# One weight row taken past the second expert product: precomputed token factors in a fused linear attention and soft mixture of experts kernel

## The chip, the cores and the metric

The kernel runs on one core of a Trainium2 chip. The metric is the device time of one execution in microseconds (us); the median of several executions counts. The profile is one execution recorded by the hardware profiler; its span (119.8 us before the change) runs from the first to the last instruction and is a little shorter than the device time of the same execution (121.55 us).

## The reference

Two layers run one after the other. The first is a linear attention with a decaying state for 4 batches, 8 heads, 768 tokens and head size 48. Its output, seen as `x` of 3072 tokens by 384 features, feeds a soft mixture of 8 experts with 4 slots each:

```python
logits = x @ phi                              # 3072 x 32
d = exp(logits - max over tokens); d /= d.sum(0)
slot_input = (d.T @ x).reshape(8, 4, 384)
for e in range(8):
    h = np.maximum(slot_input[e] @ w1[e], 0.0)   # 4 x 1024
    slot_out[e] = h @ w2[e]                      # 4 x 384
c = exp(logits - max over slots); c /= c.sum(1)
out = c @ slot_out.reshape(32, 384)           # 3072 x 384
```

The last line is linear in `slot_out`, and `slot_out` of one expert is a sum over the 1024 rows of its `w2`. So the contribution of some rows of `w2` can be added either to `slot_out` or, after a product with the token weights, straight to `out`. That is what the change uses.

## The kernel before

Everything is one straight program; the helper `O` keeps every engine's instructions in the order in which they are written. The attention and the dispatch part of the mixture fill the span up to about 90 us and are not touched. The change concerns what follows.

**Weights.** All expert weights are loaded by GpSimd-issued transfers that convert float32 to bfloat16 on the way: eight pieces `w1_all[:, e]`, then `w2` of experts 0 to 6 whole, and `w2` of expert 7 in three pieces (L576, L577). The 1024 rows of one `w2` lie as 128 partitions by 8 "rows" `y`, so piece `(y0, y1)` carries rows `y0` to `y1 - 1` of every partition. `w2` of all experts lands in the tiles `raw`.

**First expert product** (L619 to L631). The hidden values of 4 experts at a time (group `g`, 32 partitions per expert) go into two banks of PSUM per group, named by `hb`; ScalarE or VectorE applies the maximum with zero and writes `h_sb`. TensorE transposes `h_sb` (L648) into `hT`.

**Second expert product** (`second`, L656). It adds, for each row `y`, each half `x` of the 384 columns and each expert `j`, one product of 32 stationary columns by 192 columns into the banks `SO[0]` (tile `Xb`) and `SO[1]` (tile `Yb`). The order is: group 0, experts 4 and 5, one filler product `busy(1)` (L144), expert 6, expert 7. Expert 7 comes last because its weights land last.

**Slot outputs.** After it come four small products that sum token weights (`row_sums(8, 12)`, L637), then `so` (L671 on VectorE, L672 on ScalarE), which scales the two banks by `csr`, the reciprocal of the column sums of `d`, and writes bfloat16.

**Output** (`emit`, L682). There are 24 output tiles; tile `i` holds tokens `i, i + 24, ...` in 128 partitions by 384 columns. One TensorE product of the transposed token weights `LexpT[:, i:Nn:nN]` (128 by 128) with `so` fills one of six PSUM banks, and VectorE (even tiles, L686) or ScalarE (odd tiles, L688) scales it by the reciprocal row sum `rsr` into SBUF. The first two tiles are cut into two halves so that both engines work on them. After tile 5 and after tile 11 stand six more `row_sums` products with their reciprocal (L641).

Finished tiles leave in groups of 1, 1, 2, 2, 2, 4, 4, 4 and 4 tiles, one transfer each (L704). Groups 1, 2, 3, 5, 7 and 9 are issued by SyncE, groups 4, 6 and 8 by GpSimd:

```python
sizes = [1, 1, 2, 2, 2, 4, 4, 4, 4]
...
O((sp, pool)[gi % 2 if gi > 1 else 0].dma_start(out=out_v[:, i0:i, :], in_=o_s))
```

Of the kernel before, what the change touches and what calls it, by code (L numbers as in the profile page):

```python
# [9 lines left out]
def kernel(  # L10
# [14 lines left out]
    C = 128  # L25
    nC = S // C
    Nn, Dm = out.shape
    ES = moe_phi.shape[1]
    E = moe_w1.shape[0]
# [3 lines left out]
    nF = F // C  # L33
# [5 lines left out]
    nN = Nn // C  # L39
# [6 lines left out]
    f32 = mybir.dt.float32  # L46
    bf = mybir.dt.bfloat16
    i32 = mybir.dt.int32
    AF = mybir.ActivationFunctionType
    ALU = mybir.AluOpType  # L50

    def O(ins):
        return tc.keep_in_program_order(ins)

    pe, dve, act, pool, sp = nc.tensor, nc.vector, nc.scalar, nc.gpsimd, nc.sync

    big = ctx.enter_context(tc.tile_pool(name="big", bufs=1))
    cst = ctx.enter_context(tc.tile_pool(name="cst", bufs=1))
# [6 lines left out]
    EG = E // 2  # L65
    raw = [big.tile([128, 3 * RW], f32, name=f"raw{j}") for j in range(NR)]
    eW2 = nF * Dm
    w1_all = big.tile([128, E, nM, F], bf, name="w1_all")

    def w2_of(e):  # L70
        g, j = divmod(e, EG)
        return raw[1 + g][:].bitcast(bf)[:, j * eW2:(j + 1) * eW2].rearrange("p (y d) -> p y d", y=nF)
# [4 lines left out]
    T0 = psb.tile([128, 1024], bf, name="T0")  # L77
    T1 = psb.tile([128, 1024], bf, name="T1")
    Ab = psb.tile([128, 2, 512], f32, name="Ab")
# [3 lines left out]
    Vb = psb.tile([128, 512], f32, name="Vb")  # L83
# [9 lines left out]
    LexpT = cst.tile([128, Nn], bf, name="LexpT")  # L93
# [39 lines left out]
    def load_w(n, y0=0, y1=nF):  # L133
        if n < E:
            O(pool.dma_start(out=w1_all[:, n, :, :],
                             in_=moe_w1[n].rearrange("(p mo) f -> p mo f", p=128)))
        else:
            O(pool.dma_start(out=w2_of(n - E)[:, y0:y1, :],  # L138
                             in_=moe_w2[n - E].rearrange("(p y) d -> p y d", p=128)[:, y0:y1, :]))

    def keep_warm(n, bank=Yb, data=None):
        data = warm if data is None else data
        for _ in range(n):
            O(pe.matmul(bank[:, 0:512], data[:, 0:128], data[:, 0:512], start=True, stop=True))  # L144
# [349 lines left out]
    for i in range(-5, nH):  # L494
# [50 lines left out]
        if i in Z_AT:  # L545
            q = Z_AT[i]
# [12 lines left out]
        if i == 6:  # L559
            for mi in range(nM):  # L560
                for j in range(nM):
# [4 lines left out]
                                start=(j == 0), stop=(j == nM - 1)))  # L566
# [6 lines left out]
            load_w(nw)  # L573
            nw += 1
    assert nw == 2 * E - 1
    for y0, y1 in ((0, 4), (4, 7), (7, 8)):  # L576
        load_w(nw, y0, y1)  # L577


# [2 lines left out]
    Ab0 = Ab[:, 0, :]  # L582

    def busy(n):
        keep_warm(n, Ab[:, 1, :], w1_all[:, 0, 0, :])
# [23 lines left out]
    csr = cst.tile([128, 1], f32, name="csr")  # L609
# [4 lines left out]
    hb = [[Ab0, Vb[:]], [Yb[:], Ab[:, 1, :]]]  # L614
    FH = F // 2
    PH = C // 2
    h_sb = [Wf[0].bitcast(bf)[:, g * F:(g + 1) * F].rearrange("p (y c) -> p y c", c=C) for g in range(2)]
    hT = [Wf[1].bitcast(bf)[:, g * F:(g + 1) * F].rearrange("p (y c) -> p y c", c=C) for g in range(2)]
    for g in range(2):  # L619
        for a in range(2):  # L620
            for mi in range(nM):
                for j in range(EG):
                    O(pe.matmul(hb[g][a][32 * j:32 * j + 32, 0:FH], uns[:, mi, g, j, :],
                                w1_all[:, g * EG + j, mi, a * FH:(a + 1) * FH],
                                start=(mi == 0), stop=(mi == nM - 1), skip_group_check=True))
            src = hb[g][a][:, 0:FH].rearrange("p (q y) -> p y q", y=nF)
            dst = h_sb[g][:, :, a * PH:(a + 1) * PH]
            if a == 0:
                O(act.activation(out=dst, in_=src, func=AF.Relu))
            else:  # L630
                O(dve.tensor_scalar(out=dst, in0=src, scalar1=0.0, scalar2=None, op0=ALU.max))  # L631

    rsr = cst.tile([128, nN], f32, name="rsr")

    def row_sums(a, z):
        for i in range(a, z):
            O(pe.matmul(Mb[:, i:i + 1], LexpT[:, i:Nn:nN], ones[:, 0:1],  # L637
                        start=(i == a), stop=(i == z - 1), skip_group_check=True))

    def row_recip(a, z):  # L640
        O(dve.reciprocal(rsr[:, a:z], Mb[:, a:z]))  # L641

    HD = Dm // 2
    NY = nF // 2
    tb = [[T0[:], T1[:]], [Ab0.bitcast(bf), Vb[:].bitcast(bf)]]
    for g in range(2):
        for y in range(nF):
            O(pe.transpose(tb[g][y // NY][:, (y % NY) * C:(y % NY + 1) * C], h_sb[g][:, y, :], ident[:]))  # L648
        O(act.copy(hT[g][:, 0:NY, :].rearrange("p y c -> p (y c)"), tb[g][0][:, 0:NY * C]))
        O(dve.tensor_copy(hT[g][:, NY:nF, :].rearrange("p y c -> p (y c)"), tb[g][1][:, 0:NY * C]))  # L650
        if g == 0:
            row_sums(0, 8)
    row_recip(0, 8)
    SO = [Xb[:, 0:HD], Yb[:, 0:HD]]

    def second(g, experts):  # L656
        for y in range(nF):
            for x in range(2):
                for j in experts:
                    O(pe.matmul(SO[x][32 * j:32 * j + 32, :], hT[g][:, y, 32 * j:32 * j + 32],  # L660
                                w2_of(g * EG + j)[:, y, x * HD:(x + 1) * HD],
                                start=(g == 0 and y == 0), stop=(g == 1 and y == nF - 1), skip_group_check=True))

    second(0, range(EG))
    second(1, range(EG - 2))
    busy(1)
    second(1, (EG - 2,))
    second(1, (EG - 1,))
    row_sums(8, 12)
    so = Wf[1].bitcast(bf)[:, 2 * F + nM * ES * 8:2 * F + nM * ES * 8 + Dm]  # L670
    O(dve.tensor_scalar_mul(so[:, 0:HD], SO[0], csr[:, 0:1]))  # L671
# [7 lines left out]
             Wf[0][:, 2 * Dm:4 * Dm]]  # L679
            + [raw[0][:, x * 4 * Dm:(x + 1) * 4 * Dm] for x in range(4)])  # L680

    def emit(i, bank, dst, x0, x1, eng):  # L682
        op = ob[bank % 6][:, 0:x1 - x0]
        O(pe.matmul(op, LexpT[:, i:Nn:nN], so[:, x0:x1], start=True, stop=True))
        if eng is dve:
            O(dve.tensor_scalar_mul(dst[:, x0:x1], op, rsr[:, i:i + 1]))  # L686
        else:
            O(act.activation(out=dst[:, x0:x1], in_=op, func=AF.Copy, scale=rsr[:, i:i + 1]))  # L688

    i = 0  # L690
    for gi, sz in enumerate(sizes):
        o_s = obuf[gi][:, 0:sz * Dm].rearrange("p (n m) -> p n m", m=Dm)
        i0 = i
        for j in range(sz):
            if i < 2:
                emit(i, 2 * i, o_s[:, j, :], 0, HD, dve)
                emit(i, 2 * i + 1, o_s[:, j, :], HD, Dm, act)
            else:
                emit(i, i + 2, o_s[:, j, :], 0, Dm, (dve, act)[i % 2])
            i += 1  # L700
            if i in (6, 12):
                row_sums(i + 6, i + 12)
                row_recip(i + 6, i + 12)
        O((sp, pool)[gi % 2 if gi > 1 else 0].dma_start(out=out_v[:, i0:i, :], in_=o_s))  # L704
# [30 lines left out]
```

The softmax here doesn't subtract the row's maximum and nothing guards it: scores larger than these inputs give would overflow.

## Time and profile before

| | before |
|---|---|
| device time, median of 3 (range) | 121.68 us (121.32 to 121.8) |
| span of the profiled execution | 119.8 us |
| busy share of the span: TensorE / VectorE / ScalarE / GpSimd | 85% / 81% / 70% / 49% |
| granted TensorE clock, mean | 0.959 of full |
| bytes moved by transfers | 31.79 MB, mean 265 GB/s |
| share of the last chain that is the wait for `w2` | 34% |

The busy shares are means over stages with quite different limits. Read the end of the span by time instead: the last weights land a little after 102 us, the slot outputs are made around 103.5 us, TensorE and the two scaling engines produce output tiles from 104 to 111 us, and the output transfers go on until 117.5 us. The last 2.3 us up to 119.8 us hold no transfer and no compute.

### The profile page before, as it was taken

How to read it: one execution, taken by the hardware profiler on the slowest of the kernel's cores; microseconds unless marked ns; L12 is line 12 of the kernel's file. 1: busy time of each engine (PE TensorE's matmuls, PEld its weight loads, DVE VectorE, ACT ScalarE, POOL GpSimd, SP SyncE). 2: the span in 40 equal slices, each digit the busy share in tenths (PEclk: the TensorE clock that was granted, in tenths of full speed). 3: DMA queues.
4: the chain of work that ended last, by engine and by line, in shares of the span. 5: the costliest groups of instructions: out<-in, count | busy, mean ns of one | idle time of the engine just before them, and what ended most of it. 6: DMA issues, size and time to landing. Idle time of an engine off the chain costs nothing.

```text
span 119.8 us, 4336 instructions
## 1 busy us (share of the span) xinstructions
PE 102.0 (85%) x1797; PEld 82.0 (68%) x1797; DVE 96.4 (81%) x187; ACT 83.9 (70%) x183; POOL 59.2 (49%) x70
## 2 busy tenths in 40 slices
PE   5994977799999999999999999999998998896000
PEld 1453866687888888889878798888785696683000
DVE  6899999999999999899999899999954420399000
ACT  4459769797988898988988997998882520398000
POOL 7328634599999999788677595011000000013000
PEclk9998699999999999999999999999999999999955
DMA  2999999999999999999999999999999998179992
GB/s 83 255 370 374 373 367 369 363 391 367 339 381 385 348 229 215 213 213 217 213 217 213 217 218 215 212 217 212 217 215 217 211 209 161 23 274 383 410 410 99
DMA packets 20925, 31.79 MB, mean 265 GB/s; under 512 B 1129, under 2 KB 17898, under 8 KB 20906
## 3 DMA queue, kind: packets, MB, share of 16 engines
q0 software_dynamic: 2960, 14.55, 55.5%
q1 hardware_dynamic: 17920, 16.96, 41.8%
q8 instruction: 14, 0.23, 0.7%
q14 instruction: 5, 0.04, 0.1%
q10 hardware_dynamic: 26, 0.00, 0.0%
HBM read 39.38 MB, written 4.72 MB: 368 GB/s over the span
## 4 chain that ended last, share of the span: by engine, by line
DMA 34%; PE 28%; DVE 17%; issue 6%; ACT 3%; POOL 3%; POOLq 0%; DVEq 0%; ACTq 0%
DMA raw<-in_moe_w_dram 34%; PE Vb L284 4%; PE T L235 3%; DVE W L188 3%; DVE prod L257 3%; PE Ab L299 3%; PE Yb L352 2%; POOL kr L228 2%; DVE AT L304 2%; PE T L247 2%; PE Mb L325 2%; DVE kn L252 2%; DVE Z L341 2%; PE Yb L144 2%; PE Yb L365 1%
## 5 line engine op out<-in xcount | busy, mean ns | idle before, releaser
L228 POOL TENSOR_TENSOR kr<-raw,W 128x576 bf16<-128x576 f32 x30 | 42.2, 1428 | 13.8 <-ACT W L192 6.2
L304 DVE TENSOR_TENSOR AT<-Ab,mask_ut 128x768 bf16<-128x768 f32 x32 | 30.3, 946 | 0.8 <-PE Ab L299 0.6
L235 PE MATMUL T<-ident,kr 128*128 128x128 bf16 x192 | 16.8, 227 | 1.8 <-POOL kr L228 1.7
L284 PE MATMUL Vb<-v_bf,Q 128*128 128x96 bf16 x288 | 17.8, 208 | 0.0
L284 PEld LDWEIGHTS <-Q 128*128 128x128 bf16 x288 | 15.9, 99 | 1.5 <-issue 0.2
L241 ACT COPY kT<-T 128x768 bf16<-128x768 bf16 x16 | 12.8, 800 | 4.6 <-PE T L235 3.3
L241 ACT COPY rT<-T 128x768 bf16<-128x768 bf16 x16 | 12.8, 801 | 4.2 <-PE T L235 3.6
L257 DVE TENSOR_TENSOR prod<-T,kT 128x768 bf16<-128x768 bf16 x16 | 15.2, 948 | 0.0
L235 PEld LDWEIGHTS <-kr 128*128 128x128 bf16 x192 | 12.5, 101 | 2.6 <-POOL kr L228 1.9
L342 DVE TENSOR_TENSOR dv<-vn,Mb 128x288 bf16<-128x288 bf16 x32 | 14.1, 440 | 0.0
L290 ACT CAST vn<-Vb 128x288 bf16<-128x288 f32 x32 | 13.4, 419 | 0.1
L341 DVE TENSOR_TENSOR Z<-Mb,zt 128x288 bf16<-128x288 f32 (+1 forms) x32 | 12.7, 397 | 0.6
L372 ACT CAST x<-Yb 128x288 bf16<-128x288 f32 x32 | 13.1, 409 | 0.1
L299 PE MATMUL Ab<-rT,kT 64*128 64x128 bf16 x192 | 11.1, 222 | 2.1 <-DVE AT L304 2.0
L704 POOL DMA_DIRECT2D out_dram<-W x1 | 0.6, 552 | 24.2 <-DVE W L686 24.2
L325 PE MATMUL Mb<-vn,kn 128*128 128x96 bf16 (+2 forms) x80 | 11.5, 242 | 0.0
L352 PE MATMUL Yb<-vn,AT 128*128 128x48 bf16 x192 | 10.3, 185 | 0.1
L270 ACT CAST v_bf<-raw 128x576 bf16<-128x576 f32 x15 | 10.2, 678 | 0.0
L299 PEld LDWEIGHTS <-kT 64*128 64x128 bf16 x192 | 5.6, 95 | 5.6 <-DVE AT L304 2.0
L352 PEld LDWEIGHTS <-AT 128*128 128x128 bf16 x192 | 7.1, 96 | 3.3
L138 POOL DMA_DIRECT2D raw<-in_moe_w_dram x10 | 5.5, 558 | 7.8 <-DMA raw<-in_moe_w_dram 7.7
L365 PE MATMUL Yb<-dv,ident 128*128 128x288 bf16 x32 | 9.1, 284 | 0.2
(143 smaller groups left out, 221.3 us busy)
## 6 DMA issues: line engine op xcount, KB each, us to landing
w_all<-in_moe_w_dram POOLq DMA_DIRECT2D x8, 768.0 KB, 12.9
raw<-in_moe_w_dram POOLq DMA_DIRECT2D x7, 768.0 KB, 18.2
raw<-in_v_dram SPq DMA_DIRECT2D x12, 288.0 KB, 6.6
raw<-in_k_dram SPq DMA_DIRECT2D x8, 288.0 KB, 6.0
raw<-in_r_dram SPq DMA_DIRECT2D x8, 288.0 KB, 6.2
raw<-in_k_dram SPq DMA_DIRECT2D x2, 1152.0 KB, 12.3
raw<-in_r_dram SPq DMA_DIRECT2D x2, 1152.0 KB
out_dram<-raw POOLq DMA_DIRECT2D x2, 768.0 KB, 6.9
```

The source lines that it names most:

```text
L228: O(eng.tensor_mul(kr[:, j].rearrange("p j (h s) -> p j h s", s=64)[:, :, :, 0:D], src, W[j][:, q].rearrange("p j (h d) -> p j h d", h=2)))
L235: O(pe.transpose(bank[:, x * C:(x + 1) * C], kr[:, j, x, :], ident[:]))
L241: O(act.copy(t[:].rearrange("p (s j) -> p s j", j=J), bank[:, 0:S].rearrange("p (j s) -> p s j", j=J)))
L257: O(dve.tensor_mul(pr[:].rearrange("p (s j) -> p s j", j=J), T1[:, 0:S].rearrange("p (j s) -> p s j", j=J), st["kT", m][:].rearrange("p (s ...
L284: O(pe.matmul(Vb[:, c * P2:(c + 1) * P2], Q3[:, o:o + C], vb[:, :, g, j, :], start=(j == 0), stop=(j == JV - 1)))
L290: O(act.copy(vn[:].rearrange("p c e d -> p (c e d)"), Vb[:, 0:L * P2]))
L299: O(pe.matmul(Ab[:, e, c * C:(c + 1) * C], kT[s, t], rT[s, t]))
L304: O(dve.tensor_mul(AT[:], Ab[:, :, 0:T].rearrange("p e (c t) -> p e c t", c=L), mask_ut[:, None, None, :].to_broadcast([128, 2, L, C])))
L325: O(pe.matmul(o, kn[:, g * L + c, :], vc, start=first, stop=True, skip_group_check=True))
L341: O(dve.tensor_mul(Z[:], Mb[:, 0:x * P2].rearrange("p (c e) -> p c e", c=x), zt[:, q, 0:x, :]))
L342: O(dve.tensor_mul(dv[:], st["v", i][:].rearrange("p c e d -> p (c e) d"), Mb[:, 288:288 + 2 * L, None].to_broadcast([128, L * 2, D])))
L352: O(pe.matmul(Yb[:, o:o + D], AT[:, e, c, :], vn[:, c, e, :], start=first, stop=False, skip_group_check=True))
```

## The change

The last row (`y = 7`) of expert 7's `w2` no longer passes through the second expert product. Instead:

- `hs` holds the hidden values that multiply this row (those of the last 32 partitions, scaled by `csr`), made by two small ScalarE instructions (`hs_half`) from the same PSUM banks as before.
- `g_last(q)` multiplies `hs` with the token weights in token order, 512 tokens at a time; the six results, 128 partitions by 3072 tokens, go as bfloat16 into `gl`, which takes the place of expert 7's `w1`. ScalarE copies three of them out of PSUM and VectorE three. The first takes the place of `busy(1)`, the other five stand between experts 6 and 7.
- `second` for expert 7 runs over rows 0 to 6 only.
- Every output tile becomes the sum of two products in one PSUM bank: first `gl` of its tokens with row 7 of `w2`, then, as before, the token weights with `so`. For the first two tiles the four half-tile products of the first kind are issued ahead of all products of the second kind; from tile 2 on the two stand together.
- The three pieces of the last expert's `w2` become 5, 2 and 1 rows in place of 4, 3 and 1.

The purpose is that the piece of weights that lands last need not go through the second product and the scaling into `so` before output can start.

```diff
-    for y0, y1 in ((0, 4), (4, 7), (7, 8)):
+    for y0, y1 in ((0, 5), (5, 7), (7, 8)):
         load_w(nw, y0, y1)
...
+    last = slice(32 * (EG - 1), 32 * EG)
+    hs = cst.tile([128, C], bf, name="hs")
+
+    def hs_half(a):
+        O(act.activation(out=hs[last, a * PH:(a + 1) * PH], in_=hb[1][a][last, nF - 1:FH:nF], func=AF.Relu,
+                         scale=csr[last, 0:1]))
+
+    hs_half(0)
+    gl = w1_all[:, E - 1, :, :].rearrange("p m f -> p (m f)")
+    GW = 512
+    gbank = [Ab[:, 1, :], T0[:].bitcast(f32), T1[:].bitcast(f32), Ab0, Vb[:], Ab[:, 1, :]]
+
+    def g_last(q):
+        O(pe.matmul(gbank[q], hs[last, :], LexpT[last, q * GW:(q + 1) * GW], start=True, stop=True))
+        dst = gl[:, q * GW:(q + 1) * GW]
+        if q % 2:
+            O(dve.tensor_copy(dst, gbank[q]))
+        else:
+            O(act.copy(dst, gbank[q]))
...
+    hs_half(1)
     row_recip(0, 8)
...
-                                start=(g == 0 and y == 0), stop=(g == 1 and y == nF - 1), skip_group_check=True))
+                                start=(g == 0 and y == 0),
+                                stop=(g == 1 and y == nF - 1 - (j == EG - 1)), skip_group_check=True))
 
     second(0, range(EG))
     second(1, range(EG - 2))
-    busy(1)
+    g_last(0)
     second(1, (EG - 2,))
-    second(1, (EG - 1,))
+    for q in range(1, 6):
+        g_last(q)
+    second(1, (EG - 1,), range(nF - 1))
     row_sums(8, 12)
...
-    def emit(i, bank, dst, x0, x1, eng):
+    def emit(i, bank, dst, x0, x1, eng, first=True, then=True):
         op = ob[bank % 6][:, 0:x1 - x0]
-        O(pe.matmul(op, LexpT[:, i:Nn:nN], so[:, x0:x1], start=True, stop=True))
+        if first:
+            O(pe.matmul(op, gl[:, i:Nn:nN], w2_of(E - 1)[:, nF - 1, x0:x1], start=True, stop=False))
+        if not then:
+            return
+        O(pe.matmul(op, LexpT[:, i:Nn:nN], so[:, x0:x1], start=False, stop=True))
...
+    for i in range(2):
+        for x in range(2):
+            emit(i, 2 * i + x, None, x * HD, (x + 1) * HD, None, then=False)
...
-                emit(i, 2 * i, o_s[:, j, :], 0, HD, dve)
-                emit(i, 2 * i + 1, o_s[:, j, :], HD, Dm, act)
+                emit(i, 2 * i, o_s[:, j, :], 0, HD, dve, first=False)
+                emit(i, 2 * i + 1, o_s[:, j, :], HD, Dm, act, first=False)
```

More of the change, by code (lines that the diff above doesn't have):

```diff
@@ L652, with second @@
             row_sums(0, 8)
+    hs_half(1)
     row_recip(0, 8)
     SO = [Xb[:, 0:HD], Yb[:, 0:HD]]
-    def second(g, experts):
-        for y in range(nF):
+    def second(g, experts, ys=range(nF)):
+        for y in ys:
             for x in range(2):
```

## The prediction

> **What bounds the kernel now.** I read the chain that ended last first, in order of time, because the change concerns only the end of the span. Columns are start, length and what was running.
>
> ```profile
> 77.84 24.80 DMA raw<-in_moe_w_dram
> 102.64 0.04 issue
> 102.68 0.24 PE Xb L660
> ...
> 103.33 0.10 PE Xb L660
> 103.43 0.02 issue
> 103.46 0.43 DVE W L671
> 103.89 0.04 issue
> 103.93 0.33 PE T L684 x2
> ```
>
> The middle piece of the last `w2` (rows 4 to 6) lands at 102.64 us and releases TensorE; eight products follow at about 0.082 us each (102.68 to 103.25), so row 7 must have landed by 103.17 without being waited for. VectorE makes half of `so` in 0.43 us, and the first output product starts at 103.93 us.
>
> Second, the transfers from 105 to 113 us, in slices of 0.2 us:
>
> ```profile
> DMA  0009999999999999999599919989899989899979
> GB/s 0 0 8 338 353 323 353 361 415 415 384 369 461 354 323 415 384 384 569 215 461 492 430 62 461 399 338 430 369 461 461 399 338 430 338 492 461 369 307 399
> ```
>
> From 105.6 us on, the output transfers keep all transfer engines busy, except for one hole, at 109.6 us (62 GB/s). Windows cut at that hole (from and to, length, busy time of TensorE, its weight loads, VectorE, ScalarE and GpSimd, granted clock, transfer share, GB/s):
>
> ```profile
> 105.40:107.40 2.00, 2.00 (x18) 1.85 (x18) 2.00 (x6) 2.00 (x6) 0.55 (x1) 1.00 0.90 332
> 107.40:109.60 2.20, 1.97 (x10) 1.13 (x8) 2.20 (x6) 2.20 (x6) 0.53 (x1) 1.00 1.05 408
> 109.60:109.80 0.20, 0.20 (x2) 0.00 (x0) 0.20 (x2) 0.20 (x1) 0.00 (x0) 1.00 0.19 62
> 109.80:113.80 4.00, 0.03 (x1) 0.00 (x0) 1.07 (x3) 0.65 (x2) 0.53 (x1) 0.94 1.01 406
> 113.80:117.40 3.60, 0.00 (x0) 0.00 (x0) 0.00 (x0) 0.00 (x0) 0.00 (x0) 0.50 1.02 418
> ```
>
> Groups 1 to 5 are 8 tiles of 196,608 bytes. Groups 6 to 9 are the other 16, 3.15 MB, and start at 109.8 us; at about 410 GB/s they take 7.7 us, which gives the 117.5 us where transfers stop. So the end is set by when group 6 (tiles 8 to 11) can start. Third, the timeline around it:
>
> ```profile
> 105.75 0.33 PE L684 MATMUL Xb<-W,LexpT 128*128 128x384 bf16 x1
> 105.91 0.33 PE L684 MATMUL Yb<-W,LexpT 128*128 128x384 bf16 x1
> ...
> 106.89 0.58 ACT L688 ACTIVATE raw<-T,rsr 128x384 f32<-128x384 f32 x1
> ...
> 107.04 0.61 DVE L686 TENSOR_SCALAR raw<-T,rsr 128x384 f32<-128x384 f32 x1
> ...
> 108.22 0.53 POOL L704 DMA_DIRECT2D out_dram<-raw x1 [1.06 <-ACT raw L688]
> ```
>
> TensorE gives a tile every 0.16 us; VectorE needs about 0.525 us per even tile (107.04 to 107.65 is tile 10), ScalarE about 0.47 per odd one (106.89 to 107.47 is tile 11). Tile 10 closes group 6 at 107.65 us, GpSimd's record starts at 108.22, and its bytes flow from 109.8, 1.6 us later. Group 4's record starts at 106.60; a window from 104.7 to 108.5 us lists SyncE's queue alone, and one from 108.5 to 109.7 lists 0.39 MB, just group 4, on GpSimd's: 2.0 us. So group 6 came at the short end of what this path takes, without visible slack: a delay of tiles 8 to 11 moves the end one for one.
>
> **What the Trainium skill says.** "TensorE: Matmul & The Clock Gate", Back-to-back issue gap, gives N / 2.4 + 2.5 ns for a warm product of N columns: 162 ns at 384, and the trace has 0.16 us. "VectorE: DVE Perf Modes", Why PSUM operands drop a tier, says a float32 operand in PSUM gets no fast mode; the trace agrees: 192 columns take 0.42 us and 384 take 0.61, about 1 ns per column. "DMA: Bandwidth & Descriptors", Issuing engines are not separate DMA queues, says that all issuers share 16 transfer engines: spreading over SyncE and GpSimd adds no bandwidth, as the steady 406 to 418 GB/s shows. Its section Latency and other measured facts has about 1 us to the first byte for GpSimd's path; the trace's 1.6 and 2.0 us are longer and are used.
>
> **The change part by part.**
>
> *Pieces of 5, 2, 1.* Same bytes. From 101.35 us (rows 0 to 3 landed, by the wait of TensorE before 101.39) to 102.64 three rows came, 0.43 us each. So rows 0 to 4 land at about 101.8, rows 5 and 6 still at 102.64, row 7 at about 103.1 (102.64 + 0.43). After 102.64 only four products of the second kind remain in place of eight: 4 x 0.082 = 0.33 us less, if TensorE is free then.
>
> *Making `hs` and `gl`.* `hs_half(0)` falls on ScalarE at 94.9, where it idles 0.36 us; about 0.25 us for 64 columns (0.42 less 128 x 1 ns, bounded by 0.42) hides there. `hs_half(1)` comes at 96.9 and ScalarE is idle until 103.5. `g_last(0)` replaces `busy(1)` one for one. Five `g_last` follow expert 6, whose last product starts at 100.73: 5 x 0.21 = 1.07 us (512 columns at the rate of the 384), plus about 0.1 us for each switch between product shapes (the 99.16 filler and the step from 103.25 to 103.43 show such gaps). TensorE waited 0.58 us there before 101.39 and 0.64 before 102.68. With the switches the five end at 101.9 to 102.1; ten products of rows 0 to 4 end at 102.7 to 102.9, four of rows 5 and 6 start then or at 102.68. So the last product of the second kind starts at 102.93 to 103.16, before at 103.25. The copies are 128 by 512: ScalarE's 0.60 and VectorE's 0.69 from the first expert product. VectorE's three, one after another from 101.3, end at 103.2 to 103.5, near the time it is needed for `so`; this may take back 0.1 us.
>
> *First products ahead.* After the last second product come `row_sums(8, 12)` (0.18 us switch, 0.25 us) and now four half products (4 x 0.082 = 0.33 us) before the first product with `so`. Before, that start was 103.25 + 0.68 = 103.93, set by `so`; now TensorE's own queue gives last start + 0.18 + 0.25 + 0.33 = + 0.76. So it is at 103.69 to 103.92, gain 0.0 to 0.24; I take 0.12, start 103.81. The new wait of the four half products for row 7 (about 103.1) is over before they come (103.4 to 103.6); behind it are queued all output products, so a late row would shift everything.
>
> *Two products for each tile.* Counted from the first product with `so`: four half products 0.33 us; tiles 2 to 5 at 2 x 0.164 = 0.33 each, 1.31; row sums 0.38 (105.00 to 105.38 before); tiles 6 to 11, 1.96. Tile 11 leaves TensorE at 3.98, is readable 0.19 later (0.33 of one product less 0.16, and a signal), ScalarE takes 0.59: group 6 closes at 4.76. Before it closed at 107.65 - 103.93 = 3.72. That is 1.04 us later; VectorE and ScalarE, at 0.47 to 0.525 for every second tile, now wait for TensorE at 0.66 for every second tile. Weight loads (0.15 us) lie beside products of 0.16. So group 6 closes at 103.81 + 4.76 = 108.57, 0.92 later than before.
>
> *Transfers.* Groups 1 to 3 start 0.1 us earlier or level. Group 5 closes at about 107.3 (before 106.6); groups 4 and 5 are through by about 110.2 even so, before group 6 begins at 109.8 + 0.92 = 110.7. Groups 7 to 9 close by about 110.3, 111.6 and 112.9, ahead of the transfers (group 6 alone takes until 112.6). End: + 0.92. SyncE and GpSimd have only issue work, no new wait. I round down for a group 6 whose slack the trace cannot exclude (up to 0.1 us): + 0.85, thus 121.68 + 0.85 = 122.5 us.
>
> **Rivals.** *The transfers hide the slower tiles.* If the hole at 109.6 is only the closing of one transfer, with group 6's descriptors ready up to about a microsecond before, only the earlier start counts: 121.68 - 0.2 = 121.5. For it: transfers need 0.48 us per tile, more than TensorE's 0.33. Against: group 4's 2.0 us say that group 6 cannot have been ready much sooner. *The start itself becomes later or the restart longer.* `gl` copies on VectorE delay `so` and the half products, and GpSimd's 2.0 us applies to group 6: + 0.1 of start in place of - 0.12, and + 0.4 of restart: 121.68 + 0.85 + 0.2 + 0.4 = 123.1. For it: TensorE has hardly any slack from 100.8 to 103.2; against: 1.6 us was seen on a queue already in use.
>
> **How the numbers follow.** Forecast 0.62, hidden transfers 0.20, longer restart 0.18. Within 0.5% is 121.07 to 122.29. The first rival lies there save for a low tail of 0.06 below 121.07; that leaves 0.14, and the low side of the forecast adds 0.13 (a start gain of 0.24 and some slack give 122.2), together 0.27. Slower: 0.67. The range 121.6 to 123.1 cuts most of the first rival's lower half and the upper half of the second.
>
> **What would show it.** Right: output products in pairs at 0.33 us per tile with VectorE and ScalarE idle between tiles; group 6's GpSimd record near 109.1 and the hole in the transfers near 109 to 110.7, wider than 0.2 us; transfers ending near 118.4; the first product with `so` near 103.8. Wrong: transfers without a wider hole, or a rate after it off 410 GB/s, or a last weight landing moved by the piece sizes.

## The result and the profile after

The changed kernel takes 123.02 us (median of 6, 122.84 to 123.85) against 121.74 us before in the same session: ratio 1.0122, 95% interval 1.0082 to 1.0163. The loss is 1.3 us by the medians and 1.5 us by the ratio. The direction was forecast; the loss is 1.6 to 1.8 times the 0.82 us forecast. The experiments show two terms wrong in opposite senses: a wait that was put at nothing, and the slower pace of the output, which was priced too high.

The recorded execution after is the longest of its kernel (123.85 us): the weights of expert 6 came late in it, and TensorE started on them at 100.44 us (99.48 before). Distances from a common event are therefore safer to read than absolute times. Here the common event is the last product of expert 6. TensorE's timeline before, with start, length, line and shapes:

```profile
100.73 0.25 PE L660 MATMUL Yb<-raw,W 128*32 128x192 bf16 x1
...
103.25 0.25 PE L660 MATMUL Yb<-raw,W 128*32 128x192 bf16 x1
...
103.93 0.33 PE L684 MATMUL T<-W,LexpT 128*128 128x192 bf16 x2
```

And after:

```profile
101.67 0.25 PE L682 MATMUL Yb<-raw,W 128*32 128x192 bf16 x1
101.85 0.60 PE L647 MATMUL T<-LexpT,hs 32*128 32x512 bf16 x2
102.30 0.37 PE L647 MATMUL Ab<-LexpT,hs 32*128 32x512 bf16 x1
102.51 0.37 PE L647 MATMUL Vb<-LexpT,hs 32*128 32x512 bf16 x1
103.67 0.37 PE L647 MATMUL Ab<-LexpT,hs 32*128 32x512 bf16 x1 [0.79 <-DVE w_all L650]
...
105.05 0.25 PE L682 MATMUL Yb<-raw,W 128*32 128x192 bf16 x1
105.23 0.44 PE L658 MATMUL Mb<-ones,LexpT 128*128 128x1 bf16 x4
105.53 0.37 PE L710 MATMUL T<-raw,w_all 128*128 128x192 bf16 x2
...
105.91 0.33 PE L713 MATMUL T<-W,LexpT 128*128 128x192 bf16 x2
```

Five factor products follow expert 6. Four run at their pace, and the sixth of all (the last) stands for 0.79 us until VectorE has copied something. VectorE's timeline says what; ScalarE's line below it is the copy of the first factor product:

```profile
102.33 0.69 DVE L650 CAST w_all<-T 128x512 bf16<-128x512 f32 x1 [5.08 <-issue]
102.94 0.68 DVE L650 CAST w_all<-Ab 128x512 bf16<-128x512 f32 x1
104.08 0.69 DVE L650 CAST w_all<-Ab 128x512 bf16<-128x512 f32 x1 [0.46 <-PE Ab L647]
105.26 0.42 DVE L696 TENSOR_SCALAR W<-Xb,csr 128x192 bf16<-128x192 f32 x1 [0.49 <-PE Xb L682]
```

```profile
99.77 0.58 ACT L652 CAST w_all<-Ab 128x512 bf16<-128x512 f32 x1 [2.37 <-PE Ab L647]
```

The copy that ends at 103.62 us reads the fourth factor product from `Ab0`, the first half of tile `Ab`. The sixth product writes `Ab[:, 1, :]`, the other half, another bank, whose own contents ScalarE had copied out by 100.35. The two share no bytes, but they share a tile (`Ab0` is `Ab[:, 0, :]`). The same pair had stood in the profile before and was passed over. The list of waits before, in the stretch from 89 to 91 us, gives who waited, for whom, and for how long in total, how often, and at longest:

```profile
PE Ab L144 <- DVE W L483: 0.5, 1, 0.5
```

There the filler product into `Ab[:, 1, :]` waits for VectorE to copy `Ab0`. After the change all of expert 7 is queued behind this wait. The last second product starts at 105.05 us, the first product with `so` at 105.91, two microseconds later than before (103.25 and 103.93). Of these, 0.94 us are the late weights of this execution (101.67 in place of 100.73). From the last product of expert 6 to the first product with `so` it is 4.24 us, before 3.20: 1.04 us come from the change.

Next, the pace. From there the products come in pairs, one product every 0.16 us, as forecast. Tile 11 and GpSimd's record of group 6:

```profile
110.11 0.58 ACT L717 ACTIVATE raw<-T,rsr 128x384 f32<-128x384 f32 x1
```

```profile
110.98 0.53 POOL L736 DMA_DIRECT2D out_dram<-raw x1 [1.76 <-ACT raw L717]
```

Group 6 closes at 110.69, 4.78 us after the first product with `so` (forecast 4.76; before 3.72). The transfers, from 107 to 115 us in slices of 0.2 us, and windows (columns as in the prediction) cut where groups change:

```profile
DMA  0009999999999299799799992978999987999998
GB/s 0 0 0 353 330 392 353 392 453 369 415 369 415 92 492 399 307 369 399 308 415 384 430 369 62 430 307 338 399 492 492 430 338 307 399 492 461 461 461 338
```

```profile
109.80:110.80 1.00, 1.00 (x11) 0.95 (x10) 0.80 (x2) 0.82 (x2) 0.00 (x0) 1.00 0.98 393
110.80:112.00 1.20, 1.20 (x10) 1.09 (x8) 1.12 (x2) 0.76 (x2) 0.53 (x1) 1.00 0.83 328
112.00:114.00 2.00, 2.00 (x14) 1.83 (x13) 1.90 (x4) 1.79 (x4) 0.00 (x0) 1.00 0.97 393
```

By the queues of the packets, group 4 fills the first window, group 5 the second up to 111.8, group 6 the third. Two slices fall below 100 GB/s (109.6 and 111.8), where there was one before. Group 6's bytes start 1.3 us after the group closes; before it was 2.15 us (107.65 to 109.8). From the first product with `so` to group 6's bytes it is 112.0 - 105.91 = 6.1 us, before 109.8 - 103.93 = 5.9. So a group that closes 1.06 us later delays its bytes by only 0.2. To the end of the span it is 122.1 - 105.91 = 16.2 us, before 119.8 - 103.93 = 15.9: the output as a whole takes 0.3 us longer. In these two traces the loss is thus about 1.04 us ahead of the output and 0.3 us in it.

### The profile page after: what moved, and what is told of

It is laid out like the page before. It is cut to its first block, busy times and chain, and to the rows that moved or that the text cites. A ratio compares the mean times of both kernels' runs of the same rounds, so it can differ in the third digit from the quotient of the medians.

```text
span 122.1 us, 4408 instructions
## 1 busy us (share of the span) xinstructions
PE 106.9 (88%) x1826; PEld 86.7 (71%) x1826; DVE 99.6 (82%) x190; ACT 86.9 (71%) x188; POOL 59.1 (48%) x70
## 4 chain that ended last, share of the span: by engine, by line
PE 70%; DVE 11%; ACT 6%; issue 5%; POOL 1%; DVEq 0%; ACTq 0%
PE T L235 8%; PE Vb L284 8%; PE Ab L299 6%; PE Yb L352 5%; PE T L247 4%; PE Mb L325 4%; PE Yb L144 3%; DVE prod L257 3%; PE Yb L365 3%; PE Xb L380 2%; PE Xb L387 2%; PE Yb L363 2%; PE Xb L682 2%; DVE AT L304 2%; PE Yb L682 2%
```

## The experiments

All ratios are to the kernel before, with 95% intervals. Line numbers of the kernels differ by a few.

**Another bank for the sixth product.** One word of the changed kernel:

```diff
-    gbank = [Ab[:, 1, :], T0[:].bitcast(f32), T1[:].bitcast(f32), Ab0, Vb[:], Ab[:, 1, :]]
+    gbank = [Ab[:, 1, :], T0[:].bitcast(f32), T1[:].bitcast(f32), Ab0, Vb[:], Mb[:]]
```

> The changed kernel with one word different: the sixth factor product goes into the idle tile Mb in place of the second half of tile Ab. Theory W (the cost is a wait: the sixth product stood until VectorE had copied the fourth out of the other half of Ab, 0.79 us, and everything after it moved): the wait is gone, the first product with so starts 0.5 to 0.8 us earlier than in the changed kernel, time 122.2 to 122.6 us, ratio to before 1.004 to 1.008. Theory P (the pace of two products per tile costs the time, through group 6): no change against the changed kernel, 123.0 us, ratio 1.012.

Measured: 122.25 us, ratio 1.0050 (1.0036 to 1.0064). The intervals of this kernel and of the changed one do not overlap; the difference of the ratios is 0.0072, about 0.9 us. Its TensorE timeline:

```profile
100.95 0.25 PE L682 MATMUL Yb<-raw,W 128*32 128x192 bf16 x1
...
101.79 0.37 PE L647 MATMUL Vb<-LexpT,hs 32*128 32x512 bf16 x1
102.00 0.37 PE L647 MATMUL Mb<-LexpT,hs 32*128 32x512 bf16 x1
...
103.39 0.25 PE L682 MATMUL Yb<-raw,W 128*32 128x192 bf16 x1
103.57 0.44 PE L658 MATMUL Mb<-ones,LexpT 128*128 128x1 bf16 x4
103.87 0.37 PE L710 MATMUL T<-raw,w_all 128*128 128x192 bf16 x2
...
104.24 0.33 PE L713 MATMUL T<-W,LexpT 128*128 128x192 bf16 x2
```

The sixth product follows the fifth after 0.21 us with no wait; after the change it was 1.16 (102.51 to 103.67), 0.95 more. The wait is shown as a cause. That it hangs on the shared tile, and not on something else about that bank, is read from this line and the one before the change; no run keeps the bank and splits the tile. What remains is 0.6 us, and this timeline holds part of it: from the last second product to the first product with `so` it is 0.85 us here (103.39 to 104.24), 0.68 before. The row sums and then four half products lie in between, so TensorE's own queue and not `so` sets this start, 0.17 us later.

**The pieces alone.** The kernel before with `((0, 5), (5, 7), (7, 8))`.

> The kernel before with the pieces of the last w2 cut 5, 2, 1 alone. Prediction's step: four products fewer after the landing of the middle piece, but two of them wait for row 7 anyway, so 0.0 to 0.16 us less: 121.5 to 121.7 us. Rival (the cut moves the landings themselves): expert 6 or row 7 lands 0.5 us or more later, 122.2 us.

Measured: 121.62 us, ratio 0.9988 (0.9968 to 1.0007). No change that can be told from none. In its trace TensorE starts on rows 0 to 4 at 101.89 and on row 7 at 103.18, close to the landings that the prediction worked out (101.8 and 103.1), and the first product with `so` starts at 103.93, as before.

**The pace alone.** The kernel before, every output product issued twice, the second overwriting the first:

```diff
-        O(pe.matmul(op, LexpT[:, i:Nn:nN], so[:, x0:x1], start=True, stop=True))
+        for _ in range(2):
+            O(pe.matmul(op, LexpT[:, i:Nn:nN], so[:, x0:x1], start=True, stop=True))
```

> The kernel before with every output product issued twice into the same bank, the second overwriting the first; nothing else. This is the pace of two products per tile alone. Theory P: group 6 closes 1.0 us later and the end moves as much, 122.6 to 122.8 us, ratio 1.008. Theory W (transfers hide the pace): end moves by 0.1 to 0.3 us with the later first groups, 121.8 to 122.0 us, ratio 1.002.

Measured: 122.44 us, ratio 1.0053 (1.0028 to 1.0078), 0.3 to 0.95 us. It lies between the theories. In its trace group 6 closes 5.11 us after the first output product (104.23 to 109.34), 1.39 us later than before and not the 1.0 that was expected, because the halves of the first tiles are doubled too; 1.39 us would be a ratio of 1.011, outside the interval. So the pace costs something, but the closing of group 6 does not pass one for one to the end. About 0.17 us of it are the halves of the first tiles, whose first transfer is issued 0.98 us after the first output product in place of 0.81. In the transfers from 105 to 113 us two slices fall below 100 GB/s, as after the change:

```profile
DMA  0000049999888999299689799992597999988999
GB/s 0 0 0 0 0 177 361 384 361 376 292 338 353 415 384 399 92 461 399 276 369 461 292 415 399 384 399 77 246 430 307 492 461 461 369 338 338 492 461 430
```

**The part before the output alone.** The changed kernel without the products of `gl` with row 7.

```diff
-        if first:
-            O(pe.matmul(op, gl[:, i:Nn:nN], w2_of(E - 1)[:, nF - 1, x0:x1], start=True, stop=False))
...
-        O(pe.matmul(op, LexpT[:, i:Nn:nN], so[:, x0:x1], start=False, stop=True))
+        O(pe.matmul(op, LexpT[:, i:Nn:nN], so[:, x0:x1], start=True, stop=True))
```

> The changed kernel without the products of gl with row 7, so the output leaves out row 7 of expert 7; hs, the six factor products and their copies stay. This is the part of the change that lies before the output. Theory W: it costs nearly all, 122.5 to 122.8 us (0.2 to 0.4 us less than the changed kernel, for the four half products and the pace), ratio 1.007. Theory P: back to before or just under it, 121.5 to 121.8 us, ratio 1.000.

Measured: 122.87 us, ratio 1.0082 (1.0056 to 1.0108). One product per tile, and still 1.0 us slower than before, a little above the expected range: most of the loss lies ahead of the output. The wait of 0.79 us stands in its trace too. This speaks for the wait and against the pace as the main cause.

**The same without the wait.** Both edits together: the sixth product in `Mb`, no products with row 7.

> The changed kernel with the sixth factor product in Mb and without the products of gl with row 7 (the output leaves out row 7 of expert 7). What is left is the making of hs and gl without the wait. Theory W: the five factor products and the two switches of shape move the last second product by about 0.14 us (103.39 in the run with Mb, 103.25 before), so 121.7 to 121.95 us, ratio 1.000 to 1.002; the rest of that run's 0.6 us lies in the half products ahead and in the pace. Rival (the copies of gl on VectorE and ScalarE delay so, or the late weights do): ratio 1.004 or more, as in the run with Mb.

Measured: 121.77 us, ratio 1.0007 (0.9988 to 1.0025). The kernel of the run above differs only in the bank, and the intervals do not overlap, so the wait is shown a second time: 0.0075, again about 0.9 us. Once it is gone, `hs`, the factor products, their copies and their switches of shape cost nothing that can be measured, set against the two second products that they replace. The step from here to the kernel with `Mb` and all products, 0.0043 or about 0.5 us, is what the products with row 7 cost. It fits the traces: 0.17 us for the half products ahead, and 0.3 us from the first product with `so` to the end of the span with `Mb` (16.16 us, here 15.86).

**All factor products early.** An attempt at a better version: all six ahead of expert 6, each in a bank that is free by then.

```diff
-    gbank = [Ab[:, 1, :], T0[:].bitcast(f32), T1[:].bitcast(f32), Ab0, Vb[:], Ab[:, 1, :]]
+    gbank = [Ab0, T0[:].bitcast(f32), T1[:].bitcast(f32), Vb[:], Mb[:], Ab[:, 1, :]]
...
-    g_last(0)
-    second(1, (EG - 2,))
-    for q in range(1, 6):
-        g_last(q)
+    for q in range(6):
+        g_last(q)
+    second(1, (EG - 2,))
```

> The whole change, with all six factor products ahead of expert 6, where TensorE waits for weights, and each in a bank that is free. An attempt at a better version. Theory W: the last second product starts at 103.0 to 103.2, the first product with so at 103.9 to 104.0, level with before, and the pace adds 0.2 to 0.4 us: 121.9 to 122.1 us, ratio 1.002 to 1.004. If the pace costs nothing: ratio 0.998 to 1.000.

Measured: 121.96 us, ratio 1.0015 (0.9995 to 1.0035). It lies just below the expected range. The best form of the change that was tried; level with the kernel before, not faster. It also shows the pace of the whole change by itself, since its output starts when it did before:

```profile
103.91 0.33 PE L712 MATMUL T<-W,LexpT 128*128 128x192 bf16 x2
```

```profile
108.11 0.58 ACT L716 ACTIVATE raw<-T,rsr 128x384 f32<-128x384 f32 x1
```

```profile
GB/s 0 0 38 330 361 377 361 384 438 369 415 445 353 62 492 430 276 338 430 308 430 384 399 415 31 430 369 369 369 430 492 461 338 338 338 492 492 461 399 399
```

Group 6 closes at 108.69 us, 1.04 later than before (107.65). Its bytes follow the slice with 31 GB/s, at 110.0, before at 109.8. The time is longer by 0.4 us at most (the upper end of the interval), not by 1.04.

**Where the pace costs.** The doubled product in tiles 6 to 11 alone, then in tiles 12 to 23 alone (`range(2 if 6 <= i < 12 else 1)` and `range(2 if i >= 12 else 1)`).

> The kernel before with the output product issued twice for tiles 6 to 11 alone. Group 6 closes about 0.5 us later (TensorE 6 x 0.16 us more, of which about 0.45 us was hidden behind the scaling). One for one, as the prediction had it: 122.2 us, ratio 1.004. Theory S (group 6 had about 0.6 us of slack, since GpSimd's path needs 1.0 us from its record to the first bytes and not 1.6): 121.7 to 121.8 us, ratio 1.000 to 1.001.

> The kernel before with the output product issued twice for tiles 12 to 23 alone. Both theories: groups 7 to 9 are closed long before the transfers come to them, so no change, ratio 0.999 to 1.001. If doubled products cost in another way (transfers slowed by TensorE's reads, closing of groups one after another), ratio 1.003 or more.

Measured: 1.0024 (1.0003 to 1.0045) for the middle tiles, 1.0003 (0.9980 to 1.0025) for the late ones. The late tiles show no cost that can be told from none. For the middle ones the value lies between the two theories and the interval holds both, so this pair alone doesn't size the slack of group 6.

**Smaller groups.** Tiles 8 to 11 sent as two groups of two, with the early factor products and, as a control, in the kernel before.

```diff
-    sizes = [1, 1, 2, 2, 2, 4, 4, 4, 4]
+    sizes = [1, 1, 2, 2, 2, 2, 2, 4, 4, 4]
```

> The whole change with all factor products ahead of expert 6, and in addition the first output group of four tiles (tiles 8 to 11) sent as two groups of two. Theory S (what the pace costs is that group 6 is ready too late): tiles 8 and 9 are ready about 0.65 us sooner, the hole closes, and 0.1 to 0.3 us come back against the run with the early factor products: 121.6 to 121.85 us, ratio 0.998 to 1.000. If the pace costs in another way: 121.96 us as there, ratio 1.0015 or more.

> The kernel before with the same regrouping of the output alone, as the control. Theory S: group 6 had slack before, so the regrouping brings nothing but perhaps the hole of 0.2 us: 121.6 to 121.8 us, ratio 0.998 to 1.000. If a late group 6 bound the kernel before, as the prediction had it: 0.3 us or more less, ratio 0.997 or lower.

Measured: 1.0030 (1.0016 to 1.0045) with the change, 0.9983 (0.9964 to 1.0002) without. The regrouping did not bring the pace's cost back, so the theory that this cost is only the late closing of group 6 missed. The trace says why: GpSimd's record of the smaller group 6 starts 4.42 us after the first product with `so` (5.07 with the early factor products alone), but its bytes start 6.1 us after it in both, because group 5 holds the transfers until then (110.2 us). The control agrees with slack before, though its interval does not exclude the 0.997 of the other theory.

## Why the prediction was right and wrong

**The step that failed** is "Making `hs` and `gl`": "With the switches the five end at 101.9 to 102.1". It priced the five products by their own length and the gaps between shapes and took their banks as free. The fifth of them had to wait for a copy out of the other half of its tile, 0.79 us in the trace, 0.72% of the time (1.0122 less 1.0050) when only its bank is changed. This term was set to zero. It explains more than half of the loss, and more than the distance from the forecast (1.0067, which is 0.82 of 121.68 us) to the result. The rest of the step was right: with `Mb` the last second product starts 2.44 us after the last of expert 6, which is 103.17 on the clock before, and 102.93 to 103.16 was forecast.

**Transfers.** The claim that "a delay of tiles 8 to 11 moves the end one for one" failed too. The closing of group 6 was forecast to within 0.02 us (4.76, measured 4.78), but the end follows by less: with the early factor products a closing 1.04 us later costs 0.15% (-0.05 to 0.35).

The trace before showed 1.6 us from GpSimd's record to group 6's bytes and 2.0 for group 4, and the prediction took these for what the path needs. After, where GpSimd's queue held no other group by then, the bytes start 1.0 us after the record (110.98 to 112.0). The Trainium skill, "DMA: Bandwidth & Descriptors", Latency and other measured facts, says about 1 us for this path, which the prediction set aside. The measured 1.0 agrees; since group 5 kept the transfers busy until 111.8, the path needs at most that, and the longer values before contained time behind other groups. The record itself also follows the closing sooner, 0.29 us in place of 0.57. So group 6 had slack, about 0.8 us (1.06 less 0.2).

The first rival (hidden transfers) had this right in kind, not in full: the output as a whole takes 0.3 us longer, and doubled products cost 0.53% (0.28 to 0.78) in the kernel before. With 0.3 us in this term the forecast would have been a loss of about 0.2 us (an estimate: 0.3 less the 0.12 gained at the start), so that it came as near as it did is in part luck. Which part of the 0.3 us is the one more hole between transfers and which the later groups is read off single traces, and since the regrouping recovered nothing, it stays open.

**First products ahead.** Forecast 0.76 us from the last second product to the first with `so`, measured 0.85 and 0.86. The direction, that TensorE's queue takes over from `so`, was right; the size was 0.1 short (0.30 for the row sums and 0.38 for the half products, where 0.25 and 0.33 were taken).

**Pieces, copies, `hs`.** Forecast as hidden or worth 0.1 us, which the runs agree with: 0.9988 for the pieces, 1.0007 for all of it without the wait.

**The second rival** (a later start) named the right place, the start itself, but for the wrong reasons: copies that delay `so`, and a longer restart of the transfers. Neither is in the trace: VectorE's last copy ends at 104.77, and its part of `so` starts only at 105.26, after a wait for TensorE; from record to bytes group 6 took 1.0 us, not more than before.

The saving that the change was for did not come even without the wait. Before, TensorE waited about 0.6 us twice ahead of its last products; five factor products and their switches fill that time, so with `Mb` the last second product comes only 0.08 us sooner after expert 6 (2.44 against 2.52), and the half products ahead take back more than that: 3.29 against 3.20 to the first product with `so`.

## What to carry to other kernels

Before new work is put into a bank, look in the trace for waits of that tile on the other half of the same tile: one such line, 0.5 us and off the critical path, announced this change's largest cost in advance. A delay from record to bytes that contains queueing is not a floor; take it where the queue is empty, or a step looks as if it had no slack. And work that is "made ahead" in a stage where the engine is nearly full, as TensorE was here (busy for 6.1 of the 7 us from 96 to 103 before the change), uses up the waits whose removal was the purpose.

## What the hardware showed unexpectedly

After the change, output transfers of the two queues ran one after another from group 4 to group 7, with a slice of 0.2 us below 100 GB/s at some changes of group (92 and 62; 92 and 77 with doubled products), against about 400 on either side. Before the change, groups of both queues interleaved from 109.8 us on, at 406 to 418 GB/s without such a hole. That the groups interleave when they are ready together is likely but was not tested. And a kernel's recorded execution can differ from its median by more than the effect studied: the run without the wait and without row 7's products has a median of 121.77 us and a recorded execution of 122.77 us, in which TensorE waited 1.31 us for expert 6's weights.
